# Reordering the last two groups of a decode-attention kernel, and moving a quarter of its output projection

## The chip, the cores and the metric

The kernel runs on one core of a Trainium2 chip. The metric is the device time of one execution, in microseconds (us), taken over several executions. The profile of an execution gives its span (first to last instruction of the program), which is about 1.8 us shorter than the timed value.

An execution is labelled slow when it is over 1.5% above the fastest of the same kernel, and fast otherwise. The limit is taken for each label by itself. The four later sets of rounds ran on four different chips, in each set with all kernels on the same one.

## The reference, cut to what matters

One token for each of 8 sequences; 16 query heads share 8 key/value heads; the window is the last 1024 positions; a head has 256 channels. A small MLP runs beside it, and a gate mixes the two.

```python
q = (x @ wq).reshape(B, Sq, Hq, Dh)                 # 8 x 448 @ 448 x 4096
k = repeat(k_cache[:, :, Sk - W:, :], rep)          # W = 1024, bf16
v = repeat(v_cache[:, :, Sk - W:, :], rep)
p = softmax(einsum("bhqd,bhkd->bhqk", q, k) * Dh ** -0.5)
o = einsum("bhqk,bhkd->bhqd", p, v)
a = o.reshape(B, Sq, Hq * Dh) @ wo                  # 4096 x 448
return g * a + (1 - g) * mlp(x)
```

Keys and values are 67 MB of the 77.7 MB that have to be read, and each byte is used once. The output weight `wo` is 3.7 MB, and is loaded last.

## The kernel before: the parts that matter

The 64 pairs of sequence and key/value head are handled in 16 groups of four, numbered 0 to 15. One group passes through these helpers. The engine is in the comment. PE is TensorE (matrix products), DVE is VectorE and ACT is ScalarE. In the timelines the groups of instructions of each engine come in the order in which the program recorded them, so work can only be moved in time by recording it elsewhere.

```python
turn_keys(u, half)  # DVE:  transpose the keys of a group, two halves of 2.3 us
scores(u, half)     # PE:   foreign (1) and q.k (8 matmuls of 512 columns)   -> S
top(u)              # DVE:  maximum over a row                               -> mx, m
share(u)            # PE:   the four heads' shared maximum                   -> mz
expo(u)             # DVE, ACT: exponential of the scores                    -> E, rowsum
turn(u)             # DVE:  transpose of the exponentials                    -> ET
total(u)            # PE:   sum of the exponentials                          -> den
invert(u)           # DVE, ACT: 1/sum, as selector                           -> rb, rsel
values(u)           # PE: 16 matmuls with the values (PO); ACT: first half   -> first
gather(u)           # DVE:  second half added                                -> os_
finish(u)           # PE: 2 float32 products, 4 records (fin); ACT: copy     -> oT
```

The loop keeps a lag of two groups between scores and values. Its end is written out by hand:

```python
    u = NQ - 1                      # 15
    turn(u - 1)
    total(u - 1)
    top(u)
    share(u)
    gather(u - 2)
    finish(u - 2)
    invert(u - 1)
    expo(u)
    values(u - 1)
    turn(u)
    total(u)
    invert(u)
    gather(u - 1)
    A_ps = ps_misc.tile([P, DO], F32, tag="misc", name="A_ps")
    nc.vector.memset(A_ps[:], 0.0)
    finish(u - 1)
    ...                             # cut: definitions of spread_rows and project
    HALF = NHQ // 2
    spread_rows(0, HALF)            # PE: 16 small matmuls (pp); DVE: copy -> oP
    values(u)
    gather(u)
    finish(u)
    spread_rows(HALF, NHQ)
    for q in range(NHQ):
        project(q)                  # PE: 32 matmuls, one quarter of wo  -> A_ps
    ...                             # cut: mix with the MLP, four stores
```

All large loads go through a ring of nine slots of 2 MB in one queue. The plan puts the values of groups 14 and 15 and then `wo` at the end. `wo` comes in four quarters, the last of them in three pieces.

## Time and profile before

| | before |
|---|---|
| time, median of 3 | 192.33 us (192.12 to 195.7) |
| the profiled execution | 192.88 us, span 191.1 us |
| read from HBM | 77.68 MB, 407 GB/s over the span |
| DMA engines | 90% or more in 37 of 40 slices |

The page of the profile, three of its rows of busy tenths (40 slices of 4.8 us each; PEclk is the granted clock of the TensorE, in tenths of full speed) and the two lines of the chain that ended last:

```profile
PE   0035999794878489857666699859684999396773
PEclk9999657999699966999999558979998599997558
DMA  5999999999999999999999999999999999999980
...
DMA 84%; PE 7%; DVE 3%; ACT 3%; SPq 1%; issue 1%
DMA slot<-in_A_k_cache_dram 77%; DMA slot<-in_A_wq_dram 7%; PE fin L530 2%; PE A_ps L671 2%; ACT E L457 1%; PE PO L500 1%; DVE kt L356 1%; PE S L428 1%; DVE ET L470 1%; SPq L118 1%; DVE mx L440 1%; ACT first L509 0%; PE mz L448 0%; ACT oT L533 0%; PE pp L655 0%
```

The kernel is bound by its transfers, except at the end: the chain leaves the transfers with the keys of group 15 and then runs through compute instructions only. The timeline shows this end (start in us, duration, engine, line, what it writes and reads, count; in brackets how long the engine was idle before, and who ended it):

```profile
172.58 1.19 DVE L440 TENSOR_REDUCE mx<-S 128x1 f32<-128x1024 f32 x1
...
174.09 0.51 PE L448 MATMUL mz<-m,same 128*128 128x4 f32 x2 [1.74 <-DVE m L442]
174.55 1.02 PE L530 MATMUL fin<-rsel,os__1465 128*128 128x8 f32 x4
175.50 1.88 PE L500 MATMUL PO<-slot,ET 128*16 128x512 bf16 x16
175.60 0.23 ACT L533 CAST oT<-fin 128x16 bf16<-128x16 f32 x1 [3.69 <-PE fin L530]
175.67 0.30 ACT L492 ACTIVATE rsel<-sel,rb 128x8 f32<-128x8 f32 x1
175.88 1.43 ACT L457 ACTIVATE E<-S,nmx 128x1024 bf16<-128x1024 f32 x1
...
178.72 0.99 PE L530 MATMUL fin<-rsel,os__1506 128*128 128x8 f32 x4 [0.73 <-DVE os__1506 L515]
...
180.19 1.90 PE L500 MATMUL PO<-slot,ET 128*16 128x512 bf16 x15
...
183.17 1.02 PE L530 MATMUL fin<-rsel,os__1551 128*128 128x8 f32 x4 [1.08 <-DVE os__1551 L515]
...
184.67 3.18 PE L671 MATMUL A_ps<-slot,oP 128*8 128x112 bf16 x127
...
187.89 0.33 DVE L688 SCALAR_TENSOR_TENSOR res<-A_ps,gg_s,mixb 128x112 bf16<-128x112 f32 x1 [2.66 <-PE A_ps L671]
```

TensorE is idle for 1.74 us before the shared maximum's product (`mz`). Behind it stand the sums of group 13 (the first `fin`), the value product of 14 (the first `PO`) and then, on ScalarE, the exponential of 15 (`E`), which waits for a copy and a selector. The value product of 15 (180.2) comes after the sums of 14.

What the end may not undercut are the landings. The DMA view (KB of one issue and us from issue to landing) of the last loads of `wo`:

```profile
slot<-in_A_wo_dram SPq DMA_DIRECT2D x1, 896.0 KB, 31.0
slot<-in_A_wo_dram SPq DMA_DIRECT2D x1, 448.0 KB, 27.3
slot<-in_A_wo_dram SPq DMA_DIRECT2D x2, 224.0 KB, 22.9
```

With the issues at 153.52, 158.42 and 163.31 us they land at 184.6, 185.7 and 186.2 us, and the trace's semaphore records put the very last piece at 186.74 us. The final vector instruction (`res`) starts at 187.89, 1.15 us later. The values of 14 land at 173.1 us and those of 15 at 178.0 us.

The granted clock of that execution, from the windows view (stretch; busy us and instructions of PE, PEld, DVE, ACT, POOL; granted clock; DMA share; GB/s):

```profile
160.56:163.97 3.41, 1.97 (x9) 0.76 (x8) 0.66 (x1) 1.52 (x3) 0.00 (x0) 1.00 0.99 423
...
170.79:174.21 3.42, 1.68 (x10) 0.80 (x8) 2.23 (x4) 1.12 (x2) 0.00 (x0) 1.00 1.02 436
174.21:187.86 13.65, 11.18 (x208) 7.99 (x208) 2.86 (x10) 3.44 (x9) 0.00 (x0) 0.50 0.82 332
```

The whole end, from just after the start of the shared maximum's product (174.09 us), ran at half clock.

### The profile page before, as it was taken

To read this page: it belongs to the slowest core of one execution; us is meant where nothing else is said; L and a number is where in the kernel's file an instruction comes from. 1 tells how busy PE (TensorE), PEld (TensorE's weight loads), DVE (VectorE), ACT (ScalarE), POOL (GpSimd) and SP (SyncE) were. 2 spreads that over 40 slices of the span, in tenths; PEclk is the share of its full clock that TensorE was granted. 3 is DMA by queue.
4 is the path that set the end of the run, shared out by engine and by line. 5 is a ranking of instruction groups with operands and counts; after the bars stand their busy time and mean duration, and the time that the engine had idled before them with its cause. 6 is when DMAs were issued, how large, how long until landed. Compare 5 with 4: busy or idle time off the path is not lost.

```text
span 191.1 us, 2508 instructions
## 1 busy us (share of the span) xinstructions
PE 135.0 (71%) x1022; PEld 69.5 (36%) x1022; DVE 128.0 (67%) x186; ACT 43.1 (23%) x91; POOL 5.0 (3%) x7
## 2 busy tenths in 40 slices
PE   0035999794878489857666699859684999396773
PEld 0021864341424143424242254315331534144452
DVE  7876465995949494949493949494949585865310
ACT  2032220313040304040404013403140034042310
POOL 8100000000000000000000000000000000000000
PEclk9999657999699966999999558979998599997558
DMA  5999999999999999999999999999999999999980
GB/s 193 411 425 429 423 434 430 418 429 425 432 432 425 418 429 432 436 422 425 425 425 434 425 429 429 425 432 422 429 425 432 432 422 429 422 436 419 407 320 7
DMA packets 6734, 77.85 MB, mean 407 GB/s; under 512 B 945, under 2 KB 1346, under 8 KB 1986
## 3 DMA queue, kind: packets, MB, share of 16 engines
q1 hardware_dynamic: 6512, 77.67, 96.1%
q8 instruction: 8, 0.13, 0.3%
q10 hardware_dynamic: 210, 0.02, 0.1%
q14 instruction: 4, 0.03, 0.1%
HBM read 77.68 MB, written 0.01 MB: 407 GB/s over the span
## 4 chain that ended last, share of the span: by engine, by line
DMA 84%; PE 7%; DVE 3%; ACT 3%; SPq 1%; issue 1%
DMA slot<-in_A_k_cache_dram 77%; DMA slot<-in_A_wq_dram 7%; PE fin L530 2%; PE A_ps L671 2%; ACT E L457 1%; PE PO L500 1%; DVE kt L356 1%; PE S L428 1%; DVE ET L470 1%; SPq L118 1%; DVE mx L440 1%; ACT first L509 0%; PE mz L448 0%; ACT oT L533 0%; PE pp L655 0%
## 5 line engine op out<-in xcount | busy, mean ns | idle before, releaser
L356 DVE STREAM_TRANSPOSE kt<-slot 128x2048 int32<-128x2048 int32 x32 | 73.7, 2305 | 35.8 <-DMA slot<-in_A_k_cache_dram 35.8
L428 PE MATMUL S<-kt,qw 128*128 128x512 bf16 x256 | 71.0, 424 | 29.9 <-DVE kt L356 27.6
L428 PEld LDWEIGHTS <-qw 128*128 128x128 bf16 x256 | 26.7, 104 | 69.8 <-issue 48.9
L457 ACT ACTIVATE E<-S,nmx 128x1024 bf16<-128x1024 f32 x16 | 22.2, 1390 | 3.0 <-DVE nmx L454 3.0
L533 ACT CAST oT<-fin 128x16 bf16<-128x16 f32 x16 | 3.6, 227 | 82.2 <-PE fin L530 82.2
L500 PE MATMUL PO<-slot,ET 128*16 128x512 bf16 x256 | 20.9, 456 | 0.0
L440 DVE TENSOR_REDUCE mx<-S 128x1 f32<-128x1024 f32 x16 | 19.0, 1185 | 0.0
L509 ACT ACTIVATE first<-PO,own 128x256 f32<-128x256 f32 x16 | 7.6, 473 | 28.6 <-PE PO L500 28.5
L470 DVE STREAM_TRANSPOSE ET<-E 128x512 int32<-128x512 int32 x16 | 11.2, 697 | 4.2 <-ACT E L457 4.2
L422 PE MATMUL S<-place,foreign 128*128 128x512 bf16 x32 | 13.4, 418 | 0.1
L448 PE MATMUL mz<-m,same 128*128 128x4 f32 x32 | 6.8, 283 | 5.9 <-ACT oT L533 4.1
L481 PEld LDWEIGHTS den<-rowsum,rowden 128*128 128x128 f32 x32 | 7.2, 231 | 4.5 <-issue 1.4
L448 PEld LDWEIGHTS mz<-m,same 128*128 128x128 f32 x32 | 5.6, 215 | 7.3 <-ACT oT L533 5.3
L500 PEld LDWEIGHTS <-ET 128*16 128x16 bf16 x256 | 5.6, 96 | 5.5 <-issue 2.7
L422 PEld LDWEIGHTS <-foreign 128*128 128x128 bf16 x32 | 3.2, 101 | 9.4 <-issue 7.6
L481 PE MATMUL den<-rowsum,rowden 128*128 128x1 f32 x32 | 5.2, 233 | 0.0
L492 ACT ACTIVATE rsel<-sel,rb 128x8 f32<-128x8 f32 x16 | 4.7, 296 | 0.7 <-DVE rb L491 0.7
L413 DVE CAST qw<-qp 32x512 bf16<-32x512 f32 x4 | 2.7, 687 | 3.2 <-ACT qw L411 3.2
L370 PE MATMUL Sq<-slot,xT 128*8 128x512 bf16 x32 | 3.5, 558 | 1.7 <-DMA slot<-in_A_wq_dram 1.7
L291 POOL MEMSET qw<- 128x5120 bf16 x1 | 4.4, 4364 | 0.0
L442 DVE TENSOR_SCALAR m<-block,mx 128x4 f32<-128x4 f32 x16 | 3.7, 229 | 0.6
L454 DVE TENSOR_REDUCE nmx<-mz 128x1 f32<-128x4 f32 x16 | 2.3, 144 | 2.2 <-PE mz L448 2.1
(135 smaller groups left out, 84.7 us busy)
## 6 DMA issues: line engine op xcount, KB each, us to landing
slot<-in_A_v_cache_dram SPq DMA_DIRECT2D x16, 2048.0 KB, 36.8
slot<-in_A_k_cache_dram SPq DMA_DIRECT2D x15, 2048.0 KB, 39.1
slot<-in_A_wo_dram SPq DMA_DIRECT2D x3, 896.0 KB, 31.0
slot<-in_A_k_cache_dram SPq DMA_DIRECT2D x2, 1024.0 KB, 7.2
slot<-in_A_wq_dram SPq DMA_DIRECT2D x1, 2048.0 KB, 11.5
slot<-in_B_w_dram SPq DMA_DIRECT2D x1, 1568.0 KB
slot<-in_B_w_dram SPq DMA_DIRECT2D x1, 1344.0 KB
slot<-in_A_wq_dram SPq DMA_DIRECT2D x1, 1024.0 KB, 13.3
```

The source lines that it names most:

```text
L291: nc.gpsimd.memset(qw[:], 0.0)
L356: nc.vector.transpose(kt[:].rearrange("p c k x r -> p (c k x r)").bitcast(WORD), kn[:, hf * CH * Dh : (hf + 1) * CH * Dh].bitcast(WORD),)
L422: nc.tensor.matmul(S[u][:, cols], lhsT=foreign[:], rhs=place[:], start=True, stop=False)
L428: nc.tensor.matmul(S[u][:, cols], lhsT=qw[:, j, u, m * RQ : m * RQ + P], rhs=kt[:, :, k, :, par], start=False, stop=(k == NK - 1 and par = ...
L440: nc.vector.reduce_max(mx[:], S[u][:], axis=AXIS.X)
L448: nc.tensor.matmul(mz[:], lhsT=same[:], rhs=m4[:], start=True, stop=True)
L457: nc.scalar.activation(E[:].rearrange("p c x i -> p c i x"), S.pop(u)[:].rearrange("p (c i x) -> p c i x", i=PAIR, x=BLK), ACT.Exp, bias=n ...
L470: nc.vector.transpose(ET[:].rearrange("p c r i -> p (c r i)").bitcast(WORD), E[:].rearrange("p c x i -> p (c x i)").bitcast(WORD),)
L481: nc.tensor.matmul(den[u][:], lhsT=rowden[:], rhs=rowsum[:], start=True, stop=True)
L492: nc.scalar.activation(rsel[u][:], sel2[:], ACT.Copy, scale=rb[:])
L500: nc.tensor.matmul(PO[32 * t : 32 * t + PAIR * RQ], lhsT=ET[:, c, 0:RQ, :], rhs=vn[:, PAIR * c * Dh : PAIR * (c + 1) * Dh], start=(c < QUA ...
L509: nc.scalar.activation(first[:], PO[:, 0, :], ACT.Copy, scale=own[:, 0:1])
```

## The change

The intent: TensorE has a hole while DVE looks for the maximum of group 15. The sums of 13 and the value product of 14 are put into it, so that the exponential of 15 and all that follows come earlier. The first quarter of the projection is put where TensorE waits for ScalarE's copy of the last sums.

```diff
     u = NQ - 1
+    A_ps = ps_misc.tile([P, DO], F32, tag="misc", name="A_ps")
+    gather(u - 2)
+    finish(u - 2)
     turn(u - 1)
     total(u - 1)
+    values(u - 1)
     top(u)
     share(u)
-    gather(u - 2)
-    finish(u - 2)
     invert(u - 1)
     expo(u)
-    values(u - 1)
+    gather(u - 1)
+    finish(u - 1)
     turn(u)
     total(u)
     invert(u)
-    gather(u - 1)
-    A_ps = ps_misc.tile([P, DO], F32, tag="misc", name="A_ps")
     nc.vector.memset(A_ps[:], 0.0)
-    finish(u - 1)
... (cut)
     values(u)
     gather(u)
     finish(u)
+    project(0)
     spread_rows(HALF, NHQ)
-    for q in range(NHQ):
+    for q in range(1, NHQ):
         project(q)
```

No instruction is added or removed on any engine.

## The prediction

> **What bounds the kernel now.** The transfers. The page shows the 16 DMA engines at 90% or more in 37 of 40 slices, 407 GB/s over the span; the chain of waits is 84% DMA. Only the end is open. The timeline says: the last matrix product (the output projection, 128 matmuls, gap-free from 184.6 us at 25 ns each) ends at 187.87 us, the last vector instruction at 188.22, the output lands, and the span is 191.1.
>
> The trace's landing records (the DMA view gives them as issue plus time to landing) say when the last inputs arrive: values of group 14 at 173.1 us, of group 15 at 178.0, the four quarters of the output weight at 180.2, 182.4, 184.6 and, in three pieces, 185.7, 186.2, 186.7. So today compute runs 1.1 us behind the last byte. That is all that reordering compute can win: every load is issued by 168.2 us, before the changed part matters, and its slot is free long before.
>
> **What the change moves.** No instruction is added or removed on any engine (the order comparison gives equal counts); bytes are equal.
>
> Before, from the chain: maximum of 15 ends 173.78, the shared maximum's product waits to 174.6, the sums of 13 (0.99 us) come after it, the ScalarE exponential of 15 is held until 175.97 by the copy (175.60) and the selector (175.67) in front of it; the value product of 14, ready since 173.1, runs only at 175.5, at half clock for 1.88 us; the value product of 15, whose data are there at 178.0, starts at 180.15, after a chain exponential, turn, gather 14, sums 14 (0.99), copy, spread.
>
> After:
> 1. Sums of 13 at about 172.1 and the value product of 14 at 173.1 fill a hole in which TensorE is idle (1.7 us before the shared maximum's product). That product starts at about 174.2, as before.
> 2. The exponential of 15 starts near 174.9 instead of 175.97 (1.1 us earlier), its turn ends near 177.0.
> 3. The value product of 15 then waits for its data: starts at 178.0, 2.1 us earlier. Sums of 15 end near 182 instead of 184.2.
> 4. The first quarter of the projection (32 matmuls, 0.8 us) fills the 0.3 us hole while ScalarE copies the last sums. Alone it would win about 0.3 us; behind step 3 it wins nothing, because the third quarter now waits for its weight until 184.6 and the last piece until 186.7.
>
> After the last piece there remain 8 matmuls (0.2 us) and the drain: TensorE ends near 187.1 instead of 187.87. So of about 2.4 us won in compute, about 0.75 us is kept; the rest becomes a wait for the output weight.
>
> **Clock.** The windows view shows a granted clock of 1.00 to 174.2 us and 0.50 from there to 187.9. The Trainium skill, "TensorE: Matmul & The Clock Gate", Part 1, says that a free-running window of about 3.4 us with little activity halves the clock; the trace agrees, its clock pieces are multiples of 3.41 us. Filling the hole at 172 to 174 us may keep full speed one window longer. Since the end then waits for transfers, I expect almost no time from it.
>
> **Predicted:** 191.6 us against 192.33 (span about 190.3), range 191.0 to 192.3; within 2% at 0.97, faster 0.01, slower 0.02.
>
> **What would show it.** Right: value product of 15 starts within 0.3 us of 178.0; TensorE waits on the weight's transfers before the third quarter; last matmul at 187.0 to 187.3; landings unchanged. Wrong: value product of 15 later than 179, or no wait in the projection.
>
> **What would make it wrong.** Landings that shift with the order of work; ScalarE or PSUM buffers holding the exponential longer than I think, so that compute still ends last; one slow execution in three (195.7 is there before) moving a median.

## The result, and the profile after

Ratios and their intervals use fast runs alone, and are not exactly the ratio of the means or medians that are quoted beside them.

| | before | changed |
|---|---|---|
| median of 4 | 192.27 us | 192.16 us (191.94 to 192.35) |
| ratio of fast runs | | 0.9997, 95% interval 0.9977 to 1.0016 |
| profiled execution | 192.88 us, span 191.1 | 191.94 us, span 190.2 |
| `res` starts | 187.89 us | 186.96 us |
| last landing of `wo` | 186.74 us | 186.51 us |

The two traces differ by what was predicted, and the two medians hardly differ. Both need explaining. First the same rows of the page of the changed kernel, and the first line of its chain:

```profile
PE   0037799896848775796669874848396839687572
PEclk9999999999996999699975999999799987999555
DMA  5999999999999999999999999999999999999990
...
DMA 77%; PE 12%; DVE 7%; SPq 1%; ACT 1%; issue 1%
```

The timeline of its end:

```profile
171.76 0.53 PE L530 MATMUL fin<-rsel,os__1456 128*128 128x8 f32 x4
...
172.89 1.04 PE L500 MATMUL PO<-slot,ET 128*16 128x512 bf16 x16 [0.39 <-DMA slot<-in_A_v_cache_dram]
...
173.95 0.36 PE L448 MATMUL mz<-m,same 128*128 128x4 f32 x2
...
174.60 1.39 ACT L457 ACTIVATE E<-S,nmx 128x1024 bf16<-128x1024 f32 x1
...
175.12 0.61 PE L530 MATMUL fin<-rsel,os__1499 128*128 128x8 f32 x4 [0.81 <-DVE os__1499 L515]
...
177.78 1.88 PE L500 MATMUL PO<-slot,ET 128*16 128x512 bf16 x16 [1.02 <-DMA slot<-in_A_v_cache_dram]
...
180.82 1.03 PE L530 MATMUL fin<-rsel,os__1551 128*128 128x8 f32 x4 [1.15 <-DVE os__1551 L515]
181.77 0.92 PE L671 MATMUL A_ps<-slot,oP 128*8 128x112 bf16 x32
...
184.34 0.92 PE L671 MATMUL A_ps<-slot,oP 128*8 128x112 bf16 x32 [0.77 <-DMA slot<-in_A_wo_dram]
...
186.55 0.36 PE L671 MATMUL A_ps<-slot,oP 128*8 128x112 bf16 x8 [0.21 <-DMA slot<-in_A_wo_dram]
```

The window before its clock drops, from the windows view:

```profile
172.92:176.33 3.41, 2.22 (x24) 1.38 (x23) 1.80 (x6) 2.17 (x5) 0.00 (x0) 1.00 0.97 411
```

Both value products now wait for their transfer. The sums of 15 start at 180.82 instead of 183.17, 2.35 us earlier. But the third quarter of the projection then waits 0.77 us for its weight, and the last piece again. The chain that ended last shows the same in its last pieces (start, us, what):

```profile
167.97 18.54 DMA slot<-in_A_wo_dram
186.51 0.04 issue
186.55 0.38 PE A_ps L671 x8
...
186.96 0.33 DVE res L689
```

A good measure of the end is therefore how long after the last landing `res` starts: 1.15 us before, 0.45 us after. That is 0.70 us, and the other 0.23 us of the 0.93 us between the traces is a transfer stream that was earlier in this execution.

The medians are another matter. The profiled execution of before took 192.88 us; its timed executions took 192.12 to 192.33, leaving out 195.7. So the trace showed an execution worse than these three. That these had little to lose is concluded from their times; none of them was traced.

### The profile page after: what moved, and what is told of

Read it like the earlier page. It is cut to its first block, busy times and chain, and to the rows that moved or that the text cites. A ratio compares the mean times of both kernels' runs of the same rounds, so it can differ in the third digit from the quotient of the medians.

```text
span 190.2 us, 2502 instructions
## 1 busy us (share of the span) xinstructions
PE 128.5 (68%) x1013; PEld 67.1 (35%) x1022; DVE 128.0 (67%) x186; ACT 43.1 (23%) x91; POOL 5.0 (3%) x7
## 4 chain that ended last, share of the span: by engine, by line
DMA 77%; PE 12%; DVE 7%; SPq 1%; ACT 1%; issue 1%
DMA slot<-in_A_k_cache_dram 40%; DMA slot<-in_A_v_cache_dram 20%; DMA slot<-in_A_wo_dram 10%; DMA slot<-in_A_wq_dram 7%; PE S L428 6%; DVE kt L356 5%; PE hT L553 2%; PE hT L543 1%; DVE mx L440 1%; SPq L118 1%; SPq L134 1%; PE Sq L370 1%; PE qt L385 1%; ACT qs L380 1%; PE qp L398 1%
## 5 line engine op out<-in xcount | busy, mean ns | idle before, releaser
L428 PE MATMUL S<-kt,qw 128*128 128x512 bf16 x256 | 70.2, 421 | 34.5 <-DVE kt L356 30.1
L500 PE MATMUL PO<-slot,ET 128*16 128x512 bf16 x256 | 18.3, 410 | 1.4 <-DMA slot<-in_A_v_cache_dram 1.4
L422 PE MATMUL S<-place,foreign 128*128 128x512 bf16 x23 | 9.2, 400 | 0.1
L448 PE MATMUL mz<-m,same 128*128 128x4 f32 x32 | 6.2, 265 | 4.1 <-ACT oT L533 4.1
L481 PEld LDWEIGHTS den<-rowsum,rowden 128*128 128x128 f32 x32 | 6.7, 214 | 3.3 <-issue 1.0
L448 PEld LDWEIGHTS mz<-m,same 128*128 128x128 f32 x32 | 5.0, 195 | 6.0 <-ACT oT L533 5.3
L671 PE MATMUL A_ps<-slot,oP 128*8 128x112 bf16 x128 | 4.0, 290 | 1.2 <-DMA slot<-in_A_wo_dram 1.2
```

What stands on the lines that cost most here:

```text
L422: nc.tensor.matmul(S[u][:, cols], lhsT=foreign[:], rhs=place[:], start=True, stop=False)
L428: nc.tensor.matmul(S[u][:, cols], lhsT=qw[:, j, u, m * RQ : m * RQ + P], rhs=kt[:, :, k, :, par], start=False, stop=(k == NK - 1 and par = ...
L448: nc.tensor.matmul(mz[:], lhsT=same[:], rhs=m4[:], start=True, stop=True)
L481: nc.tensor.matmul(den[u][:], lhsT=rowden[:], rhs=rowsum[:], start=True, stop=True)
L500: nc.tensor.matmul(PO[32 * t : 32 * t + PAIR * RQ], lhsT=ET[:, c, 0:RQ, :], rhs=vn[:, PAIR * c * Dh : PAIR * (c + 1) * Dh], start=(c < QUA ...
```

## The experiments

Theory 1: where the clock of TensorE drops decides how far compute lags behind the landings at the end of the kernel before. The changed kernel has enough slack not to care, and is held by the landings of `wo`. Two rivals: the changed kernel gives its gain back by later landings; or something else than the weight holds its end.

### The two kernels again, and each part alone

`before_again` and `after_again` are the two kernels without an edit. The parts:

```diff
# reorder_only: against the changed kernel
-    project(0)
     spread_rows(HALF, NHQ)
-    for q in range(1, NHQ):
+    for q in range(NHQ):
# project_only: against the kernel before
+    project(0)
     spread_rows(HALF, NHQ)
-    for q in range(NHQ):
+    for q in range(1, NHQ):
```

> The kernel before, unchanged: what two equal kernels differ by, and a second trace of it. Theory 1 (clock phase): the profiled execution of before took 192.88 us, its usual ones 192.1 to 192.3, because the half clock happened to cover its whole end (174.2 to 187.9 us). In a usual execution the clock is full for part of the end, compute keeps up with the loads, and the last matmul ends within 0.3 us of the last landing of the output weight (186.7 in that trace), instead of 1.1 after it. Ratio 1.000 within 0.002. Rival (the loads of the changed kernel are later in usual executions): the last matmul of this trace too ends 1 us after the last landing, whatever the clock.

> The changed kernel, unchanged, with more rounds on the same chip. Theory 1: 0 to 0.4 us faster than before in the mean (ratio 0.998 to 1.000), last matmul 0.4 us after the last landing whatever the clock. Rival: ratio about 1.000 with the last landing later than in before by as much as was won.

> Only the reordering of groups 14 and 15; the first quarter of the projection stays behind the last spread. Both theories: the same time as the changed kernel within 0.1 us, since the third quarter waits for its weight anyway (0.77 us in the trace of the changed kernel); the wait before the third quarter shrinks to about 0.4 us.

> Only the first quarter of the projection moved between the last sums and the last spread. In an execution with the half clock over the whole end: 0.3 us faster than before in the same clock (the hole of 0.32 us while ScalarE copies is filled); with a full clock in the end: nothing. Ratio 0.998 to 1.000; the value product of group 15 still starts after 179 us.

| label | fast runs | ratio to before | 95% interval | `res` after last landing, in the trace |
|---|---|---|---|---|
| before_again | 192.75 to 195.44 us (6 of 6) | 1.0076 | 1.0030 to 1.0122 | 1.13 us |
| after_again | 191.97 to 192.32 us (6 of 6) | 0.9974 | 0.9952 to 0.9996 | 0.45 us |
| reorder_only | 191.78 to 192.47 us (6 of 6) | 0.9969 | 0.9946 to 0.9993 | 0.45 us |
| project_only | 191.88 to 194.45 us (4 of 6) | 0.9999 | 0.9960 to 1.0038 | 2.30 us |

The fast runs of the kernel before in the same rounds took 192.02 to 193.54 us (11 of 13).

The kernel before has no single time. The same program against itself came out at 1.0076, which my expectation of 0.002 missed. Part of that is the labelling: executions of 195.21 and 195.44 us count as fast in `before_again`, one of 195.26 us counts as slow in the rounds of before. With one limit for both, the means are 193.57 and 192.73 us, a ratio of 1.004. Fast executions with the reordering lie within 0.7 us of each other (191.78 to 192.47); those without it are spread over 3.6 us (191.88 to 195.44). The reordering alone has the whole effect. The moved quarter alone has none that this measurement can tell. `after_again` (0.9974) fell just below the 0.998 that I had expected. In these traces the rival of later landings falls: the last piece of `wo` landed at 186.51 and 186.53 us in two executions of the changed kernel, and at 186.74 and 186.90 in two of the kernel before.

The trace of `project_only` is of an unlucky but fast execution (194.45 us). The windows view of it, and two pieces of its chain:

```profile
165.93:169.34 3.41, 3.33 (x8) 1.30 (x8) 3.37 (x6) 0.00 (x0) 0.00 (x0) 0.50 1.05 447
```

```profile
166.01 3.52 PE S L428 x8
...
189.38 0.33 DVE res L689
```

Half clock lay on the first half of the scores of the last group, whose 8 matmuls took 3.52 us instead of 1.90 in the profile of before, and from 176.17 us again on the whole end. Everything after the scores came about 1.9 us later than in the profile of before (the shared maximum's product at 176.00 against 174.09 us), 0.3 us of it because the scores also started later, and `res` started 2.30 us after the last landing.

The trace of `before_again` has its drop at 174.48 us, nearly where the profile of before has it (174.21), and took nearly as long: 193.03 against 192.88 us. It did not show a usual execution as I had expected.

The kept traces of all kernels without reordering or filler, two of them from an experiment further below, can be lined up by where the clock dropped. Where it dropped at 174.2 to 174.5 us (`before`, `before_again`, `project_half`), the sums of 15 start at 183.17, 183.32 and 182.75 us. Where half clock lay on 165.8 to 169.3 us and again from 176.1 us on (`project_only`, `before_half`), they start at 185.10 and 184.94 us, about 2 us later. So the place of the drop goes with the time.

### Keeping the clock up without changing the order

```diff
# before_warm: against the kernel before; filler(n) = n matmuls of 128x400 into
# unused columns of A_ps's bank, read by nobody
         turn_keys(u, 0)
+        if u >= NQ - 2:
+            filler(10)
         scores(u, 0)
...
     total(u - 1)
+    filler(8)
     top(u)
...
     gather(u - 1)
+    filler(2)
...
     values(u)
+    filler(4)
     gather(u)
```

> The kernel before with idle holes of TensorE filled by matmuls whose result nobody reads (10 before the first half of the scores of groups 14 and 15, 8 before the shared maximum's product of 15, 2 before the sums of 14, 4 before the sums of 15; each 128x400, 0.17 us at full clock). Nothing of the order changes. Theory 1 (the kernel before loses its time when the half clock falls on its end): the trace shows full clock from about 163 us to the end or nearly, the last matmul ends within 0.5 us of the last landing, the times lie together within 191.8 to 192.6 like those of the changed kernel; ratio 0.994 to 0.998. Rival (the order itself costs the time, the clock is a bystander): the spread of 192.0 to over 195 stays, ratio 1.00 or above.

Measured: 191.95 to 193.00 us (6 of 6 fast, median 192.34), against 192.43 to 195.24 us (median 193.73, 11 of 11 fast) of the kernel before in the same rounds; ratio 0.9922 (0.9875 to 0.9968). The windows view:

```profile
171.57:174.98 3.41, 2.97 (x19) 1.71 (x17) 2.67 (x6) 0.38 (x2) 0.00 (x0) 1.00 1.02 432
174.98:178.40 3.42, 2.07 (x24) 0.94 (x24) 1.30 (x4) 2.37 (x6) 0.00 (x0) 1.00 0.95 397
```

TensorE was busy 2.97 us of the window that ends near 175 us, where before it was busy 1.68 us, and the clock stayed full for another window, to 178.40. The value product of 14 took 1.04 us instead of 1.88, and `res` started 0.57 us after the last landing instead of 1.15. The ratio alone would not do, since the kernel before against itself was off by as much (1.0076). The times say more: all six lie at or below 193.00 us, and 9 of the 11 of the kernel before in the same rounds lie above. Useless work made the kernel before faster, without any change of order. With the full clock on the value product of 14 in the trace, this makes the clock a cause and not a bystander; how much of the spread it explains is not measured. The clock did drop from 178.40 us to the end, which I had not expected, and the spread is 1.05 us, more than the 0.8 us I had written down; filling holes does not replace the reordering.

### How much slack the changed kernel has

```diff
# after_late2 and after_late6: against the changed kernel; the last gather is
# computed 3 and 7 times, into the same tile
     values(u)
-    gather(u)
+    gather(u, 3)        # 7
```

> The changed kernel with the last gather done three times in place of once: 0.96 us more on the chain behind the last value product (0.48 us each in the trace). Theory 1 (the end waits for the output weight; by the trace, 128 matmuls from 181.8 us would be done at about 185.4 against 186.9, so 1.4 us of slack at half clock): the time stays, within 0.15 us of the changed kernel (192.1). Rival (compute still ends last): 0.9 us more, 193.0.

> The same with the last gather done seven times: 2.9 us more on the chain. Theory 1: the slack of 1.4 us is used up and the rest shows, 1.3 to 1.7 us more than the changed kernel (193.5 us), less by up to 1 us where the clock is full in the end. Rival: 2.9 us more, 195.0.

| label | added to the chain | fast runs | median | `res` after last landing |
|---|---|---|---|---|
| after_again | 0 | 191.97 to 192.32 us | 192.21 us | 0.45 us |
| after_late2 | 0.96 us | 192.07 to 192.54 us | 192.32 us | 0.45 us |
| after_late6 | 2.9 us | 193.40 to 193.91 us | 193.54 us | 1.56 us |

The chain of `after_late2` ends in the same way as that of the changed kernel, with the weight:

```profile
187.15 0.38 PE A_ps L672 x8
...
187.56 0.33 DVE res L690
```

A microsecond more of compute was free. Of 2.9 us, 1.3 us showed in the median (193.54 less 192.21, from two sets of rounds), so about 1.6 us went into slack; at half clock I had worked out 1.4. The rival that compute still ends last falls.

### Taking the weight's transfer away

These four give a wrong result on purpose: only the first half of `wo` is loaded, and used for both halves. The compute engines do the same work; the last landing is 4.3 us earlier (at 182.4 us in the trace of `before_half`).

```diff
-    for q in range(0, NHQ, 2):         # the plan of loads
+    for q in range(0, 2, 2):
...
-        w = slot("wo", q - q % 2)
+        w = slot("wo", 0)
```

> Wrong result on purpose: the kernel before with only the first two quarters of the output weight loaded, and used twice, so that the last landing is at about 182.3 us and no longer bounds the end; the instructions on the compute engines are the same. Theory 1: no faster than before in an execution with the half clock over the end (last matmul 187.9 in the trace), at most 1 to 2 us faster than before in one with full clock.

> Wrong result on purpose: the reordering alone, with half of the output weight. Theory 1: the hidden gain of the reordering shows, 1.8 to 2.4 us faster than before_half in the same clock: last matmul near 185.8 us with the half clock (sums of 15 end at 181.8, then 0.9 of copy and spread, 3.1 of projection).

> Wrong result on purpose: the moved first quarter alone, with half of the output weight. Theory 1: 0.3 us faster than before_half in the same clock, no more.

> Wrong result on purpose: the changed kernel with half of the output weight. Theory 1: 2.1 to 2.7 us faster than before_half in the same clock, 1.2 to 1.5 us faster than the changed kernel with all of its weight (last matmul near 185.5 instead of 186.9). Rival (something else than the weight holds the end): the same time as the changed kernel.

| label | fast runs | mean | last matmul in the trace |
|---|---|---|---|
| before, same rounds | 192.19 to 195.06 us (10 of 11) | 193.71 us | |
| before_half | 192.60 to 195.08 us | 194.20 us | 189.64 us |
| project_half | 192.44 to 194.44 us | 193.28 us | 187.00 us |
| reorder_half | 190.81 to 192.91 us | 191.71 us | 186.61 us |
| after_half | 190.59 to 191.72 us | 190.97 us | 185.17 us |

The kernel before does not get faster when its last 1.8 MB are not loaded (1.0033, interval 0.9974 to 1.0092): compute ends it. The changed kernel does, to 190.97 us from the 192.19 us that its fast runs took in other rounds. The means are 3.2 us apart (194.20 less 190.97). This is the gain in compute, most of which the weight's landing hides in the real kernel. The two parts came out at 2.5 us (`reorder_half`, expected 1.8 to 2.4) and 0.9 us (`project_half`, expected 0.3), from six executions each that are spread over 2 us.

The traces of `before_half` and `after_half` happen to have the half clock on the first half of the scores of group 15 alike (165.81 to 169.22, and 165.60 to 169.01 us). Their chains, in this order, at the same places:

```profile
165.78 3.57 PE S L428 x8
...
182.15 1.72 PE PO L500 x15
...
186.61 3.03 PE A_ps L671 x126
```

```profile
165.50 3.51 PE S L428 x8
...
178.54 1.24 PE PO L500 x16
...
182.91 2.25 PE A_ps L671 x96
```

With the same bad start the reordered kernel starts its last value product 3.4 us earlier (first matmul at 178.53 against 181.92 us) and its last matmul ends 4.5 us earlier (189.64 against 185.17), not the 2.1 to 2.7 us that I expected. It also keeps the full clock longer, to 179.25 us instead of 176.05 us, so that its last two value products took 1.04 and 1.23 us instead of 1.88 and 1.94. I had costed only the moved work. The traced execution of `before_half` took 195.08 us, with its last matmul 7.2 us after its last landing: a bad phase of the clock is enough for such a time, without late transfers.

For the moved quarter the stretch from the start of the last sums to the last matmul is the cleanest reading, as it is at half clock in all four of these traces: 4.70 us before (183.17 to 187.87) and 4.69 in `before_again`, 4.25 in `project_half` and 4.26 in `project_only`. So it is worth 0.44 us there; I had expected 0.3.

### The changed kernel once more

> The changed kernel once more, since the kernel before ran at 192.3, 192.8, 193.7 and 194.1 us in the median of four sets of rounds. Theory 1: the changed kernel is again at 192.0 to 192.5 us in every execution, with a spread under 0.6 us, and the ratio (0.990 to 1.000) moves only with the kernel before. Rival (the sets differ by chip, and the changed kernel differs with them): the changed kernel too is at 193 us or above where the kernel before is.

Measured: 192.09 to 192.78 us (6 of 6 fast), against 192.28 to 194.68 us (6 of 11 fast) of the kernel before; ratio 0.9936 (0.9885 to 0.9987). The changed kernel stayed where it was while the kernel before moved, though one execution lies above the 192.5 us that I had set as a limit, and the spread was 0.69 us and not under 0.6. The five executions of the kernel before that count as slow (196.08 to 196.66 us) are left out of the ratio; they may be the far end of the same spread, but none was traced. The trace fell into a bad phase. Its windows view, and the end of its chain:

```profile
166.45:173.28 6.83, 6.51 (x33) 3.28 (x31) 4.30 (x7) 1.12 (x4) 0.00 (x0) 0.50 1.00 427
```

```profile
168.20 18.53 DMA slot<-in_A_wo_dram
...
186.77 0.36 PE A_ps L671 x7
...
187.15 0.33 DVE res L689
```

Half clock from 166.45 us covers most of the first half of the scores of group 15, as in `project_only`, and lasts twice as long. The value product of 15 started 1.57 us after its data had landed (179.54 against 177.97 us). Still `res` started 0.43 us after the last landing: the slack took it all.

Over the four later sets of rounds, 38 of the 46 executions of the kernel before were fast, at 192.02 to 195.24 us. All 16 of the changed kernel, in the first set and two later ones, were fast, at 191.94 to 192.78 us. No experiment pointed to a version that is faster than the changed kernel: the spreads of `reorder_only` and of the changed kernel overlap, and 0.45 us after the last landing is little more than the last 8 matmuls.

## Why the prediction was right or wrong

The number was right: 192.16 us lies between 191.0 and 192.3, and the change is within 2%. The mechanism at the end was right. The expected size against the timed value was not: 0.7 us were forecast, and the medians differ by 0.11. That the number was right says little, and is in part luck: the range also holds the 192.27 us of the kernel before itself.

- **Steps 1 and 2 were right.** The value product of 14 ran at 172.89 us (predicted 173.1), the shared maximum's product at 173.95 (174.2), the exponential of 15 at 174.60 (174.9).
- **Step 3 was right for this trace.** The value product of 15 started at 177.78 us, 0.04 us after its data. In a bad phase it does not: 179.54 in the trace of `after_third`.
- **Step 4 was right for the whole change**: the moved quarter adds nothing, as `reorder_only` shows. Its size by itself is 0.44 us and not 0.3.
- **The cap by the output weight was right.** `res` starts 0.45 us after the last landing; it was 1.15. The 0.70 us between them are the predicted 0.75. "About 2.4 us won in compute" was 2.35 in the trace. The last matmul ended at 186.94 us, a little before the 187.0 to 187.3 named, since the landings were not unchanged but 0.23 us earlier.
- **The step that failed is the sum "191.6 us against 192.33".** It subtracts a gain read from one execution from the median of others. The traced execution had taken 192.88 us, which was there to be read beside the profile. 192.88 less 0.75 is 192.1, which is what the changed kernel takes. The kernel before at 192.1 to 192.3 us had almost nothing left to win against that. In the later sets its fast runs averaged 192.73 and 193.38 us, and those of the changed kernel 192.19 and 192.34: 0.54 and 1.04 us.
- **The paragraph on the clock was right about the changed kernel and missed the kernel before.** I asked whether the change would keep the full clock longer, and concluded that it would matter little, as the end waits for transfers. I did not ask what the half clock did to the reference that I compared with. `before_warm` shows that it mattered: ratio 0.9922 with nothing reordered.
- **"One slow execution in three moving a median"** was named as a risk. It is more than that: fast executions alone are spread over 3.2 us (192.02 to 195.24), and the traces of `before_again` and `project_only` show intermediate cases.

What stays open: what exactly the clock monitor counts. TensorE's busy time does not settle it: in the kernel before the clock stayed full after a window with 1.97 us of busy TensorE (160.56 to 163.97) and dropped after one with 1.68; in the changed kernel it dropped at 176.33 us, after one with 2.22. Nor is there a trace of a lucky execution of the kernel before. That it ends close to the landings is concluded from its fastest times (192.02, span 190.2, as the changed kernel's) and from `before_warm`.

## What to carry to other kernels

Before subtracting a gain read in a trace from a median, compare the traced execution's own time with the median, and look at the granted clock over the stretch that the change touches. Where a reordering at the end is capped by the last landing, cost it as "the time from the last landing to the end, before and after", and look for the rest as slack: here it did not make the good executions faster, but in the traces kept it removed the dependence on where a clock window falls. Repeat a kernel against itself before believing a ratio of under one percent: here that gave 1.0076.

## What the Trainium skill lacked or had wrong

- "TensorE: Matmul & The Clock Gate", Part 1, says of the warm-up that "the ramp penalty is <1% of a typical kernel span". That is about the start of a kernel; it says nothing of a half-clock window at the end. Here the fast executions of one kernel are spread from 192.02 to 195.24 us, 1.7%, and filling holes of TensorE alone brought 0.8% (`before_warm`). What a half-clock window costs depends on whether it falls on the chain that ends last: 1.6 us on half of the scores of the last group (3.52 against 1.90 us), nothing measurable in the changed kernel.
- The same page, "HAM oscillation", gives the rule as no idle gaps of TensorE longer than about 3.4 us. Here the clock dropped at 174.21 us after a window of 3.42 us with TensorE busy for 1.68 us, in which the longest gap before a matmul was 1.74 us. The section after it, "A second HAM failure mode", does tell of frequent short idle times that make the clock oscillate; neither says what share of a window has to be busy.
- That Part 1 says the window is free-running, about 3.4 us long, and the clock either full or half agrees with all traces here: the complete pieces at half clock last 3.41, 6.83, 10.24 or 13.65 us, and their place differs from execution to execution.
- Part 1 says that the phase of the window changes the number of slow matmuls at the start of a kernel from run to run. What I found on no page is that a kernel with little slack at its end can therefore need more than a handful of executions: the fast executions of the kernel before averaged 192.73, 193.91, 193.71 and 193.38 us in the four later sets.
